# Staging k and q head by head in DRAM, and turning them from there in two 64-wide halves

## The chip, the cores and the metric

One core of one Trainium2 chip. The metric is the device time of one execution in microseconds (us). TensorE (PE) multiplies matrices, VectorE (DVE), ScalarE (ACT) and GpSimd (POOL) do the elementwise work, SyncE (SP) issues most of the transfers, and sixteen DMA engines move the data. GpSimd issues transfers too; those that change the number type (float32 to float16) all come from it.

## The reference

Attention with a bias by distance, followed by a two-layer network on its output. In the sizes of this case:

```python
# q, k, v: (8, 8, 576, 64) float32: 8 batch elements, 8 heads, 576 positions, 64 wide
scores = (1 / np.sqrt(64)) * np.matmul(q, k.transpose(0, 1, 3, 2))
scores = scores + bias_table[bucket].transpose(2, 0, 1)[None]   # bucket: by |i - j|
attn = softmax(scores)                                           # over the last axis
x = np.matmul(attn, v)           # then heads side by side: (4608 tokens, 512)
h = x @ w_in                     # (4608, 2048)
s = np.sin(alpha * h)
g = h + s * s / (alpha + 1e-09)
out = g @ w_out                  # (4608, 512) float32
```

The scores contract over the 64-wide head dimension, so TensorE needs k and q with that dimension on the partitions, the transpose of how they lie in DRAM.

## The kernel before, in words

The eight batch elements go through attention one after the other; the network follows some elements behind, in blocks of 512 tokens, and its matmuls are woven between those of the attention. The heads are taken in four pairs (`NP` = 4): a pair fills 128 partitions, the even head on 0 to 63, the odd one on 64 to 127.

The tiles `kT` and `qT` hold the turned k and q of one element, `[128, 4 pairs, 576]` in float16. There are two of each, used in turn by even and odd elements. For elements 0 and 1, and for q of element 2, the inputs are loaded to SBUF and turned on TensorE. For the rest (k of elements 2 to 7, q of elements 3 to 7, eleven tensors) two steps do it:

- `stage` (line 1238): a transfer issued by GpSimd reads one element's k or q from its input, casts it to float16 and writes it to a DRAM tensor `staged`, with the eight heads of one position side by side (576 rows of 512). `stage` is the only writer of it.
- `turn_staged` (line 1244): one transposing transfer issued by SyncE reads these 576 rows and writes `kT` or `qT`, whole.

After it, `corners` (line 1248) copies the last 64 positions of k into `kd`, and the score matmuls (lines 1364, 1395 and 1405) read `kT`, `qT` and `kd`.

SyncE issues in a fixed order, and its transfers go through one queue (q1): the staged turns, the transposing transfers `turn_x` (line 1478) which turn the attention's output into `xT`, the input of the network, and the stores of the results (lines 1626, 1645, 1652). GpSimd likewise issues in a fixed order (queue q0): early loads, then per element the loads of v and the two `stage` copies.

The order on each engine is written out by hand: the list `LINE` gives for every engine the sequence of its tasks, and a planner (`_Plan.run`) only walks along it. A task waits for its semaphores when its turn comes; what stands behind it on the same engine waits too. `turn_staged` of element t depends on its own `stage` and on the last score matmul of element t - 2, whose tile it overwrites:

```python
c = add("SP", 2.8, E("turn_staged", t, kind), pipe=3.3, prio=1, pkt=37, flow=True,
        deps=[staged[t, kind]] + last_qk[t - 2])
```

Of the kernel before, what the change touches and what calls it, by code (L numbers as in the profile page):

```python
# [9 lines left out]
F16 = mybir.dt.float16  # L10
# [4 lines left out]
T, H, S, D = 8, 8, 576, 64  # L15
NB, DM, FF, NT = 32, 512, 2048, 4608
NP = H // 2
# [4 lines left out]
def _blocks(sizes):  # L22

    at = [0]
    for n in sizes:
        at.append(at[-1] + n)
    assert at[-1] == NT
    return list(zip(at, at[1:]))


def _bucket_table(max_abs: int) -> np.ndarray:
    n = np.arange(max_abs)
    half = 16
    is_small = n < half
    log_ratio = np.log(np.maximum(n, 1).astype(np.float32) / half) / np.log(128 / half)
    large = half + (log_ratio * (half - 1)).astype(np.int32)
    large = np.minimum(large, 31)
    return np.where(is_small, n, large)
# [5 lines left out]
class _Ring:  # L44


    def __init__(self, n):
        self.n = n
        self.users = []
# [1031 lines left out]
class _Ops:  # L1081


    def __init__(self, ctx, tc, q, k, v, bias_table, moe_w_in, moe_w_out, moe_alpha, out):
        self.nc = nc = tc.nc
        self.q, self.k, self.v, self.out = q, k, v, out
        self.tab_in, self.w_in_in, self.w_out_in, self.alpha_in = (
            bias_table, moe_w_in, moe_w_out, moe_alpha)
        sgl = ctx.enter_context(tc.tile_pool(name="sgl", bufs=1))
        self.tp = ctx.enter_context(tc.tile_pool(name="tp", bufs=1))  # L1090
        ps = ctx.enter_context(tc.tile_pool(name="ps", bufs=1, space=bass.MemoryType.PSUM))
        self.acc = ps.tile([128, 8, 512], F32, name="acc")

        self.blk = _blocks(OPT["blk"])
        self.staged = [nc.dram_tensor(f"staged_{n}", [T, S, H * D], F16, kind="Internal")
                       for n in "kq"]
        bt = _bucket_table(256)

        cst = np.zeros((128, 784), dtype=np.float16)
        for a in range(4):  # L1100
            for y in range(488):
                cst[4 * bt[min(255, abs(y - 231 - 8 * a))] + a, y] = 1.0
            cst[a::4, 488 + a] = 1.0

        sub = np.repeat(np.eye(NB, dtype=np.float32), 4, axis=1)
        sub[NB - 1] -= 1.0
        cst[0:NB, 496:752] = sub.view(np.float16)
        cst[0:16, 752:784] = np.eye(16, dtype=np.float32).view(np.float16)
        self.cst_h = nc.inline_tensor(cst, "cst")
        self.ident_h = nc.inline_tensor(np.eye(128, dtype=np.float16), "eye")  # L1110

        self.kT = [sgl.tile([128, NP, S], F16, name=f"kT{i}") for i in range(2)]
        self.qT = [sgl.tile([128, NP, S], F16, name=f"qT{i}") for i in range(2)]
        self.kd = [sgl.tile([128, NP, 128], F16, name=f"kd{i}") for i in range(2)]
        self.vs = [sgl.tile([128, 4, H, 66], F16, name=f"v{i}") for i in range(2)]
        self.vt = [sgl.tile([128, NP, 130], F16, name=f"vt{i}") for i in range(2)]
        self.ur = [sgl.tile([128, 1088], F16, name=f"ur{i}") for i in range(OPT["nr"])]
        self.n_r = 0
        self.us = [sgl.tile([128, 320], F16, name=f"us{i}") for i in range(2)]
        self.xT = sgl.tile([128, NP, XR + 64], F16, name="xT")  # L1120
        self.toep = sgl.tile([128, H, 384], F16, name="toep")
        self.mt = sgl.tile([128, NP, 192], F16, name="mt")
        self.cst = sgl.tile([128, 784], F16, name="cst_sb")
        self.pick = self.cst[:, 0:492]
        self.ident = sgl.tile([128, 128], F16, name="ident")
        self.sub = self.cst[0:NB, 496:752].bitcast(F32)
        self.id32 = self.cst[0:16, 752:784].bitcast(F32)
        self.tab = sgl.tile([NB, H], F32, name="tab")
        self.e16 = sgl.tile([128, H], F16, name="e16")
        self.eb = sgl.tile([128, 4, H], F16, name="eb")  # L1130
        self.e_sb = sgl.tile([128, 392], F16, name="e_sb")
        self.w_in = sgl.tile([128, 4, FF], F16, name="w_in16")
        self.w_out = sgl.tile([128, NF, DM], F16, name="w_out16")
        self.a16 = sgl.tile([16, 128], F32, name="a16")
        self.alphaT = sgl.tile([128, NF], F32, name="alphaT")
        self.tmp_a = sgl.tile([128, NF], F32, name="tmp_a")
        self.inv_a = sgl.tile([128, NF], F32, name="inv_a")
        raw = self.toep[0:96].rearrange("p h n -> p (h n)").bitcast(F32)
        self.raw = [raw[:, 768 * i:768 * i + 768].rearrange("p (h n) -> p h n", h=2)
                    for i in range(2)]  # L1140
        self.blank = self.cst[:, 0:256]
        self.sums = sgl.tile([128, 2, 2, NF // 2, 256], F16, name="sums")
        self.wt = sgl.tile([128, 4, NF // 2, 256], F16, name="wt")
        self.touched = sgl.tile([1, 2], F32, name="touched")
        self.g = {}
# [91 lines left out]

    def stage(self, t, kind):
        src = (self.k, self.q)[kind]
        self.nc.gpsimd.dma_start(  # L1240
            out=self.staged[kind].ap()[t].rearrange("s (h d) -> s h d", h=H),
            in_=src[t].rearrange("h s d -> s h d"))

    def turn_staged(self, t, kind):
        dst = (self.kT, self.qT)[kind][t % 2]
        self.nc.sync.dma_start_transpose(out=dst[:, :, 0:S], in_=self.staged[kind].ap()[t])

    def corners(self, t, pairs):
        lo, hi = pairs[0], pairs[-1] + 1
# [455 lines left out]
```

## Time and profile before

| | |
|---|---|
| median of three runs | 373.29 us (373.19 to 374.27) |
| profiled execution | span 370.6 us; its own time beside the span is not given, and the median lies 2.7 us above the span |
| TensorE busy | 356.4 us (96%) |
| VectorE, ScalarE busy | 318.8 us, 318.4 us (86% each) |
| GpSimd busy | 87.9 us (24%) |
| bytes moved by DMA | 40.86 MB in 152415 packets |

The page of the profile lists the busy time of each engine, the traffic of each DMA queue, the chain of work that ended last, the costliest groups of instructions, and the issues of transfers with their time from issue to landing. A queue's share is the sum of the times of its packets over sixteen engines' time; it goes above 100% where packets overlap in an engine. Further views used below: the timeline of one engine, the instructions of one line or one tile, and the traffic in a cut of the span.

### The profile page before, as it was taken

How to read it: one execution, taken by the hardware profiler on the slowest of the kernel's cores; microseconds unless marked ns; L12 is line 12 of the kernel's file. 1: busy time of each engine (PE TensorE's matmuls, PEld its weight loads, DVE VectorE, ACT ScalarE, POOL GpSimd, SP SyncE). 2: the span in 40 equal slices, each digit the busy share in tenths (PEclk: the TensorE clock that was granted, in tenths of full speed). 3: DMA queues.
4: the chain of work that ended last, by engine and by line, in shares of the span. 5: the costliest groups of instructions: out<-in, count | busy, mean ns of one | idle time of the engine just before them, and what ended most of it. 6: DMA issues, size and time to landing. Idle time of an engine off the chain costs nothing.

```text
span 370.6 us, 10525 instructions
## 1 busy us (share of the span) xinstructions
PE 356.4 (96%) x4379; PEld 245.9 (66%) x4379; DVE 318.8 (86%) x711; ACT 318.4 (86%) x424; POOL 87.9 (24%) x105
## 2 busy tenths in 40 slices
PE   4969999999999999999999999999999999999996
PEld 3647546764666569755788987666965766745675
DVE  2679999999989998989998998899879997989733
ACT  5897999999999999999998999999899798476310
POOL 8895523085108000820050006200000000000000
PEclk9999999999999999999999999999999999999999
DMA  8999999899949954999799039907230012220014
GB/s 161 224 154 180 206 171 156 104 134 157 182 83 135 142 127 75 156 155 88 125 210 95 18 84 142 157 3 155 79 48 2 10 47 79 56 85 2 0 58 170
DMA packets 152415, 40.86 MB, mean 110 GB/s; under 512 B 134432, under 2 KB 151920, under 8 KB 152368
## 3 DMA queue, kind: packets, MB, share of 16 engines
q0 software_dynamic: 96656, 18.45, 60.2%
q1 hardware_dynamic: 55008, 21.22, 28.0%
q8 instruction: 34, 0.56, 0.6%
q10 hardware_dynamic: 704, 0.53, 0.6%
q14 instruction: 13, 0.11, 0.1%
HBM read 36.94 MB, written 15.93 MB: 143 GB/s over the span
## 4 chain that ended last, share of the span: by engine, by line
PE 87%; ACT 4%; POOL 3%; DMA 2%; DVE 2%; issue 1%; ACTq 0%; POOLq 0%; DVEq 0%
PE acc L1514 32%; PE acc L1611 26%; PE acc L1461 10%; PE acc L1405 9%; PE acc L1451 3%; PE acc L1558 3%; DMA wt<-in_k_dram 2%; PE acc L1364 2%; ACT s L1522 1%; PE acc L1395 1%; POOL mt L1292 1%; PE acc L1632 1%; DVE g L1543 1%; ACT u L1413 1%; POOL v L1219 1%
## 5 line engine op out<-in xcount | busy, mean ns | idle before, releaser
L1514 PE MATMUL acc<-xT,w_in 128*128 128x512 f16 (+3 forms) x704 | 134.2, 340 | 0.7 <-DVE g L1543 0.4
L1413 ACT ACTIVATE u<-acc 128x1024 f16<-128x1024 f32 x128 | 124.3, 1035 | 8.4 <-PE acc L1405 6.4
L1543 DVE SCALAR_TENSOR_TENSOR g<-s,inv_a,acc 128x512 f16<-128x512 f16 (+2 forms) x160 | 104.5, 691 | 8.6 <-ACT s L1527 6.5
L1522 ACT ACTIVATE s<-acc,alphaT 128x512 f16<-128x512 f32 (+2 forms) x144 | 93.2, 684 | 14.7 <-PE acc L1514 10.6
L1514 PEld LDWEIGHTS <-w_in 128*128 128x128 f16 x704 | 64.4, 98 | 55.8 <-DVE g L1543 1.8
L1611 PEld LDWEIGHTS <-g 128*128 128x128 f16 (+1 forms) x768 | 59.8, 96 | 18.0 <-issue 4.4
L1441 DVE TENSOR_TENSOR u<-u,toep 128x256 f16<-128x256 f16 (+1 forms) x128 | 59.4, 487 | 1.8 <-DMA toep<-e_sb 0.9
L1219 POOL DMA_DIRECT2D v<-in_v_dram x32 | 36.8, 1278 | 99.3 <-PE acc L1461 93.3
L1611 PE MATMUL acc<-w_out,g 128*128 128x256 f16 (+1 forms) x496 | 54.1, 271 | 0.0
L1405 PE MATMUL acc<-qT,kT 64*128 64x256 f16 x512 | 46.3, 279 | 3.9 <-DVE qT L1350 1.9
L1461 PE MATMUL acc<-v,u 128*128 128x65 f16 x1024 | 45.0, 193 | 0.1
L1527 ACT ACTIVATE s<-s 128x512 f16<-128x512 f16 (+2 forms) x67 | 41.4, 629 | 1.5
L1461 PEld LDWEIGHTS <-u 128*128 128x128 f16 x1024 | 40.6, 97 | 1.4 <-issue 0.5
L1611 PE MATMUL acc<-wt,g 128*128 128x256 f16 (+1 forms) x272 | 38.4, 272 | 0.0
L1611 PE MATMUL acc<-wt,sums 128*128 128x256 f16 (+1 forms) x272 | 34.6, 273 | 0.0
L1529 DVE TENSOR_TENSOR s<-s 128x512 f16<-128x512 f16 (+2 forms) x77 | 31.9, 422 | 2.6 <-ACT s L1522 2.3
L1472 DVE TENSOR_TENSOR xp<-acc,rden 128x256 f16<-128x256 f32 (+1 forms) x64 | 31.4, 491 | 2.2
L1405 PEld LDWEIGHTS <-kT 64*128 64x128 f16 x512 | 20.3, 96 | 16.1 <-issue 12.2
L1611 PEld LDWEIGHTS <-sums 128*128 128x128 f16 (+1 forms) x272 | 23.5, 97 | 7.9 <-issue 2.5
L1451 PE MATMUL acc<-vt,ut 128*128 128x130 f16 x128 | 28.3, 221 | 0.1
L1225 POOL DMA_DIRECT2D vt<-in_v_dram x16 | 14.1, 894 | 33.6 <-PE acc L1461 30.6
L1492 DVE COPY quarter<-acc 128x512 f32<-128x512 f32 x18 | 12.4, 687 | 9.3 <-PE acc L1611 4.7
(90 smaller groups left out, 361.6 us busy)
## 6 DMA issues: line engine op xcount, KB each, us to landing
out_dram<-quarter SPq DMA_DIRECT2D x32, 256.0 KB, 2.7
v<-in_v_dram POOLq DMA_DIRECT2D x32, 128.0 KB, 8.7
staged_k<-in_k_dram POOLq DMA_DIRECT2D x6, 576.0 KB, 10.8
staged_q<-in_q_dram POOLq DMA_DIRECT2D x5, 576.0 KB, 9.9
w_out<-in_moe_w_out_dram POOLq DMA_DIRECT2D x4, 512.0 KB, 8.7
w_in<-in_moe_w_in_dram POOLq DMA_DIRECT2D x4, 512.0 KB, 16.2
sums<-in_q_dram POOLq DMA_DIRECT2D x7, 144.0 KB, 5.6
out_dram<-outs SPq DMA_DIRECT2D x3, 256.0 KB, 2.0
```

Source lines behind the costliest of these rows:

```text
L1219: self.nc.gpsimd.dma_start(out=self.vs[t % 2][:, c, :, 0:D], in_=src)
L1405: self.nc.tensor.matmul(out=s[:, o:o + 256], lhsT=self.kT[t % 2][r, p, 128 * c:128 * c + 128], rhs=self.qT[t % 2][r, p, 256 * w:256 * w + ...
L1413: self.nc.scalar.activation(out=c["u"], in_=c["s"], func=AF.Exp, scale=0.125)
L1441: self.nc.vector.tensor_tensor(out=io, in0=io, in1=m, op=ALU.mult)
L1451: nc.tensor.matmul(out=c["av"][:, 130 * j:130 * j + 130], lhsT=tail, rhs=vt[:, p, :], start=True, stop=True, skip_group_check=True)
L1461: nc.tensor.matmul(out=c["av"][:, 130 * j + 65 * a:130 * j + 65 * a + 65], lhsT=l, rhs=vv[:, ch, 2 * p + a, 0:65], start=False, stop=True, ...
L1514: self.nc.tensor.matmul(out=c["h"][:, x:y], lhsT=self.w_in[:, j, 128 * f:128 * f + 128], rhs=self.xT[:, j, at:at + y - x], start=(j == 0 a ...
L1522: self.nc.scalar.activation(out=c["s"], in_=c["h"], func=AF.Sin, scale=self.alphaT[:, f:f + 1])
L1527: self.nc.scalar.activation(out=c["s"], in_=c["s"], func=AF.Square)
L1529: self.nc.vector.tensor_tensor(out=c["s"], in0=c["s"], in1=c["s"], op=ALU.mult)
L1543: self.nc.vector.scalar_tensor_tensor(out=o, in0=c["s"][:, x:y], scalar=self.inv_a[:, f:f + 1], in1=c["h"][:, x:y], op0=ALU.mult, op1=ALU.add)
L1611: self.nc.tensor.matmul(out=c[to][:, 256 * k:256 * k + 256], lhsT=a[r, 128 * k:128 * k + 128], rhs=b[r, :], start=to not in c["began"], st ...
```

## The change

`staged` becomes, per element, two halves (even and odd heads), and each half holds its four heads one after the other, each as 576 rows of 64: `[2, 4 * 576, 64]`. `stage` issues two copies in place of one, one for each half, with runs of 2048 numbers that are contiguous on both sides. `turn_staged` issues two transposes in place of one: each takes a half, seen as 2304 rows of 64, and writes it to 64 partitions of `kT` or `qT`, all four pairs in one row of 2304 columns. The planner's costs and the orders on the engines are the same.

```diff
-        self.staged = [nc.dram_tensor(f"staged_{n}", [T, S, H * D], F16, kind="Internal")
+        self.staged = [nc.dram_tensor(f"staged_{n}", [T, 2, NP * S, D], F16, kind="Internal")
                        for n in "kq"]
...
     def stage(self, t, kind):
         src = (self.k, self.q)[kind]
-        self.nc.gpsimd.dma_start(
-            out=self.staged[kind].ap()[t].rearrange("s (h d) -> s h d", h=H),
-            in_=src[t].rearrange("h s d -> s h d"))
+        n = S * D // 18
+        for a in range(2):
+            self.nc.gpsimd.dma_start(
+                out=bass.AP(tensor=self.staged[kind].ap().tensor, offset=(2 * t + a) * NP * S * D,
+                            ap=[[n, 18 * NP], [1, n]]),
+                in_=bass.AP(tensor=src.tensor, offset=src.offset + (t * H + a) * S * D,
+                            ap=[[2 * S * D, NP], [n, 18], [1, n]]))
 
     def turn_staged(self, t, kind):
         dst = (self.kT, self.qT)[kind][t % 2]
-        self.nc.sync.dma_start_transpose(out=dst[:, :, 0:S], in_=self.staged[kind].ap()[t])
+        for a in range(2):
+            self.nc.sync.dma_start_transpose(
+                out=dst[64 * a:64 * a + 64, :, :].rearrange("d p s -> d (p s)"),
+                in_=self.staged[kind].ap()[t, a])
```

## The prediction

> **What bounds the kernel now.** I read the page first (busy times, chain that ended last), then the waits, then what the change touches: the queues, the tiles, the timeline of SyncE.
>
> ```profile
> span 370.6 us, 10525 instructions
> PE 356.4 (96%) x4379; PEld 245.9 (66%) x4379; DVE 318.8 (86%) x711; ACT 318.4 (86%) x424; POOL 87.9 (24%) x105
> ...
> q0 software_dynamic: 96656, 18.45, 60.2%
> q1 hardware_dynamic: 55008, 21.22, 28.0%
> ...
> PE 87%; ACT 4%; POOL 3%; DMA 2%; DVE 2%; issue 1%; ACTq 0%; POOLq 0%; DVEq 0%
> ```
>
> TensorE bounds it: 356.4 of 370.6 us busy, 87% of the chain. At most 14.2 us could be gained without taking work from TensorE, and this change takes none away. So its upside is small whatever it does, and the question is whether the new transfers stay hidden. In the instructions of the two tiles and the list of transfers, the old ones are:
>
> ```profile
> L1240 POOL DMA_DIRECT2D staged_k<-in_k_dram x6: 2197/2232/2782, 37.8 to 189.6; - x6
> L1246 SPq DMA_TRANSPOSE kT<-staged_k x6: 2138/2751/4722, 55.5 to 219.0; - x6
> ```
>
> ```profile
> out_dram<-quarter SPq DMA_DIRECT2D x32, 256.0 KB, 2.7
> ...
> staged_k<-in_k_dram POOLq DMA_DIRECT2D x6, 576.0 KB, 10.8
> staged_q<-in_q_dram POOLq DMA_DIRECT2D x5, 576.0 KB, 9.9
> ...
> xT<-xp SPq DMA_TRANSPOSE x28, 2.9
> ...
> kT<-staged_k SPq DMA_TRANSPOSE x6, 5.3
> qT<-staged_q SPq DMA_TRANSPOSE x5, 5.4
> ```
>
> Eleven turns, each 5.3 or 5.4 us from issue to landing. Where they stand on SyncE (start, duration):
>
> ```profile
> 55.53 4.72 SPq L1246 DMA_TRANSPOSE kT<-staged_k  x1
> 68.55 1.20 SPq L1478 DMA_TRANSPOSE xT<-xp  x1
> 69.93 2.92 SPq L1246 DMA_TRANSPOSE kT<-staged_k  x1
> ...
> 218.98 2.29 SPq L1246 DMA_TRANSPOSE kT<-staged_k  x1
> ...
> 228.99 22.39 SPq L1626 DMA_DIRECT2D out_dram<-quarter  x3
> 251.49 2.46 SPq L1246 DMA_TRANSPOSE qT<-staged_q  x1
> ```
>
> The last turn (q of element 7) is issued at 251.49 and lands at about 256.9; the 64 score matmuls of element 7's full tiles, counted back from the end, begin at 259.2:
>
> ```profile
> L1405 PE MATMUL acc<-qT,kT x64: 269/269/280, 259.2 to 301.1; 64*128 64x256 f16 x64
> ```
>
> So the slack of that turn is 2.3 us, and behind it lie 370.6 - 259.2 = 111.4 us of work.
>
> **The stage step.** GpSimd's issue: 2.23 us each, eleven times, 24.5 us; after, 22 issues of 72 runs each. The nearest issue with few runs is a load of w_out:
>
> ```profile
> 22.14 0.78 POOL L1235 DMA_DIRECT2D w_out<-in_moe_w_out_dram  x1
> ```
>
> 22 x 0.78 = 17.2 us, a gain of 7 us on an engine that is busy 24%; bounds from -24.5 to +24.5 us, no path either way: 0. Behind each stage on GpSimd stand the v loads, which can only move by a microsecond or two. On the DMA engines the run gets longer (one packet carries 128 bytes now, 4096 then), so 11 x 4608 = 50688 of q0's 96656 packets become 22 x 72 = 1584. This too only matters if a turn waits for its stage; I take 0.
>
> **The turn step** decides. All transposing transfers of this kernel take whole units of 128 columns: 512 (4 x 128) for the staged turns, 640 (5 x 128) for `xT`. A cut inside a staged turn with nothing else in it shows the packets:
>
> ```profile
> DMA packets 792, 0.20 MB, mean 290 GB/s; under 512 B 792, under 2 KB 792, under 8 KB 792
> ## 3 DMA queue, kind: packets, MB, share of 16 engines
> q1 hardware_dynamic: 792, 0.20, 127.3%
> ```
>
> 0.20 MB / 792 = 256 bytes, one row of 128 numbers of two bytes. The cut is 0.7 us (60.5 to 61.2): 0.7 x 16 / 792 = 14.1 ns per packet on each engine. A whole turn is 2304 such packets, 144 on each engine, 2.0 us of its 5.3.
>
> The new source has rows of 64 numbers, half a unit. Nothing in the trace shows a transposing transfer with half a unit. If it isn't taken so, what is left is a plain transfer with the strides exchanged: 64 rows of 2304 numbers, in which neighbours lie 64 numbers (128 bytes) apart in DRAM. The trace shows what a plain transfer pays for: one packet for one contiguous run (64 float16 on the staged side, 128 bytes, here beside w_out's longer ones):
>
> ```profile
> q0 software_dynamic: 5664, 0.72, 126.1%
> ```
>
> 0.72 MB / 5664 = 127 bytes, in the cut from 60 to 69 us. With exchanged strides the run is one number: 64 x 2304 = 147456 packets of two bytes for each half, 9216 on each engine, against 144 before.
>
> [...]
>
> I take the exchanged strides. **The price of a two-byte packet** isn't in the trace. From below: the completion words of four bytes, 32 of them alone in a cut of 0.21 us (259.75 to 259.96):
>
> ```profile
> DMA packets 32, 0.00 MB, mean 1 GB/s; under 512 B 32, under 2 KB 32, under 8 KB 32
> ## 3 DMA queue, kind: packets, MB, share of 16 engines
> q1 hardware_dynamic: 32, 0.00, 7.0%
> ```
>
> 0.07 x 16 x 0.21 us / 32 = 7.35 ns. From above: GpSimd's queue over the whole span, 0.602 x 16 x 370.6 us / 96656 = 36.9 ns per packet, mostly 128-byte ones of the staging itself and in traffic. Between them lies the 14.1 ns of the 256-byte packets. I take 14.1 ns: same queue, same DRAM tensor as source, same destination, and I expect the packet, not its bytes, to set the price. Then one transfer takes 9216 x 14.1 ns = 129.9 us (67.7 to 340 by the bounds).
>
> [...]
>
> **What it puts on the path.** There are 22 such transfers, all in SyncE's queue, and nothing covers them: the six turns of k stand (219.0 - 55.5) / 5 = 33 us apart on average, and an element's four transfers now take 4 x 130 = 520 us. Queued behind them on SyncE and in q1 are the `xT` transposes (the network's next block waits for them on TensorE, and through TensorE's fixed order the attention too) and the stores. TensorE, VectorE and ScalarE wait at the first score matmul of each later element.
>
> - Until the first turn is issued: 55.5 us, as before.
> - 22 x 129.9 = 2858 us. Each turn's own start and landing overlap its neighbour's in the queue: 0.
> - Between elements the queue runs dry while SyncE waits for the work that stands before its next turn. In the trace of before the distance from the landing of an element's last turn to the next turn's issue is, as a bound, up to about 27 us (k of element 7: 218.98 + 5.3 = 224.3; q is issued at 251.5), taken for five places at most 135 us in all; most of that work is done now while the turns run. The 22.39 us at the three stores before q7 stay. I take 60 us, bounds 0 and 135.
> - Behind the last turn: 111.4 us.
> - Around the span: 2.7 us (373.29 - 370.6).
>
> Sum: 55.5 + 2858 + 60 + 111.4 + 2.7 = 3088 us, said as 3100. By the lower price 1490 us of transfers and 1660 us in all; by the upper one 7480 and, with 135 between, 7785, said as 7700.
>
> **The rivals.** (1) The half unit is taken as a transposing transfer: 4608 packets of 128 bytes a tensor, at 14.1 ns 288 on each engine, 4.1 us in place of 2.0, and a second issue on SyncE of 1.2 us (the shortest, `xT`'s above). A turn lands 2 to 4 us later; only q of element 7 has as little as 2.3 us. For it: the change is written with the transposing instruction. Against it: not one such transfer in the trace. Time: 373 us, between 371.5 (some of the staging's contention gone) and 376. This is the not-slower side; it decides when half a unit costs no more than a whole one, which keeps a turn within about 8 us. (2) Exchanged strides, but the sixteen engines read the same 128-byte line at the same moments, since each takes four of the 64 numbers of every line, and they hinder one another: above 36.9 ns, so over 7.7 ms. For it: in traffic, packets in q0 took 36.9 ns, 2.6 times the 14.1. [...] (3) The read side is paid below the completion words' 7.35 ns: under 1660 us. For it: packets overlap (127.3% above). Against: 7.35 ns is the shortest there is here.
>
> **How the numbers follow.** Exchanged strides inside the bounds: 0.82. Rival 2: 0.06, rival 3: 0.04, rival 1: 0.08, of which faster 0.03, same 0.04, slower 0.01. Range 1660 to 7700 us, holding the 0.82. About 0.3% is what a measurement tells from no change here; faster 0.03, same 0.04, slower 0.93.
>
> **What would show it.** Right: the entries of line 1246's successor are no longer transposing ones but plain ones; q1 has about 22 x 147456 = 3.2 million packets, two bytes each, or as many as the profiler keeps; landing in the hundreds of microseconds; TensorE's busy time still near 356 us but its share near 12%; the first large waits of TensorE are for `kT` and `qT`, and the chain goes over DMA. Wrong: transposing entries of 128-byte packets that land within 10 us (rival 1); or the stage step, if turns wait for it instead.

## The result, and the profile after

The changed kernel takes 4430.43 us (median of four runs, 4424.83 to 4449.39); the kernel before, run beside it, 373.78 us (373.19 to 374.69). The ratio is 11.86, with a 95% interval of 11.82 to 11.90. The forecast was 3100 us, between 1660 and 7700: the side and the kind of thing are right, the time is 1330 us short. The profiled execution took 4426.38 us at a span of 4424.2 us. (In the experiments "stage alone", "whole units" and "short runs" some of the four runs took 2 to 8% longer than the others at a lower clock, 0.925 to 0.970 against 0.953 to 0.982; their times below are those of the shorter ones, two, one and two of them, and from the profiles of the last two kernels, which are of a longer run, only kinds and counts are read.)

The page of the changed kernel: busy times, the granted clock over the span (one digit for each fortieth), the queues, the chain.

```profile
span 4424.2 us, 10558 instructions
PE 382.5 (9%) x4379; PEld 259.3 (6%) x4379; DVE 320.8 (7%) x711; ACT 320.7 (7%) x424; POOL 77.4 (2%) x116
...
PEclk7555555655565555555555555555555655565559
...
DMA packets 3321647, 40.87 MB, mean 9 GB/s; under 512 B 3303400, under 2 KB 3320888, under 8 KB 3321336
...
q1 hardware_dynamic: 3273696, 21.22, 178.1%
q0 software_dynamic: 47200, 18.46, 4.1%
...
another core or an unknown queue 74%; SPq 16%; PE 6%; DMA 2%; DVE 1%; POOL 0%; issue 0%; ACT 0%; DVEq 0%; POOLq 0%; ACTq 0%
```

The engines do the same work as before (TensorE 382.5 us against 356.4; the clock granted to it was 0.543 on average, 1.000 before), but it is spread over twelve times the span. The bytes are as good as the same (40.87 MB, 40.86 before). q1 has 3273696 packets where it had 55008. Take away from both the turns: before, 11 x 2304 = 25344 of 256 bytes; after, 22 x 147456 = 3244032 of two bytes. 29664 are left in both. So every turned number crosses as a packet of its own. Most of the chain stands under "another core or an unknown queue" (what the profile calls a wait it can't follow) and under SyncE's queue, in which the turns lie.

The list of transfers of the changed kernel (KB each, median us from issue to landing), and the row of the turns of k among the tile's instructions (duration of the issue in ns: shortest, median, longest):

```profile
staged_k<-in_k_dram POOLq DMA_DIRECT2D x12, 288.0 KB, 14.1
kT<-staged_k SPq DMA_DIRECT2D x12, 288.0 KB, 288.5
staged_q<-in_q_dram POOLq DMA_DIRECT2D x10, 288.0 KB, 15.9
qT<-staged_q SPq DMA_DIRECT2D x10, 288.0 KB, 376.0
```

```profile
L1251 SPq DMA_DIRECT2D kT<-staged_k x12: 607/91386/199646, 55.3 to 3527.5; - x12
```

Eleven transposing transfers have become 22 plain ones, although the kernel calls the transposing function. A landing of 288 to 376 us holds the wait behind the other half in the queue; in "one half" below, without that other half, it is 192 to 197 us. The price of one transfer by itself is read from a cut in which nothing else moves (4000 to 4100 us):

```profile
DMA packets 79792, 0.16 MB, mean 2 GB/s; under 512 B 79792, under 2 KB 79792, under 8 KB 79792
...
q1 hardware_dynamic: 79792, 0.16, 194.9%
```

0.16 MB / 79792 = 2 bytes. On each of sixteen engines a packet ends every 100 x 16 / 79792 = 20.05 ns; the share of 194.9% says that two are under way on each engine, so that one takes 39 ns. A transfer of 9216 packets on each engine takes 9216 x 20.05 ns = 184.8 us.

SyncE's timeline shows what this does to all that is queued behind (start, duration):

```profile
55.28 200.43 SPq L1251 DMA_DIRECT2D kT<-staged_k  x2
255.79 184.91 SPq L1485 DMA_TRANSPOSE xT<-xp  x1
440.88 200.24 SPq L1251 DMA_DIRECT2D kT<-staged_k  x2
641.22 187.51 SPq L1485 DMA_TRANSPOSE xT<-xp  x3
828.78 0.58 SPq L1633 DMA_DIRECT2D out_dram<-quarter  x1
829.46 188.93 SPq L1251 DMA_DIRECT2D qT<-staged_q  x2
...
4121.93 186.00 SPq L1485 DMA_TRANSPOSE xT<-xp  x2
```

An issue now lasts up to 199.6 us, as long as a whole transfer, and SyncE stands at it that long. The chain's "SPq" (16%) is this. Hence TensorE's waits, in the view of the waits (total, times, longest):

```profile
PE acc L1412 <- DMA qT<-staged_q: 1452.3, 6, 548.2
...
DVE kd L1261 <- DMA kT<-staged_k: 741.0, 4, 189.6
...
PE acc L1521 <- DMA xT<-xp: 732.6, 2, 368.1
```

TensorE waits for q (1452.3 us), for `xT` behind the turns (732.6 us), and by way of `kd` (741.0 us on VectorE) for k. The two stretches of the span in the view by windows (length, then busy time of TensorE, its weight loads, VectorE, ScalarE and GpSimd, granted clock, DMA share, GB/s):

```profile
55.30:4307.90 4252.60, 227.14 (x2638) 154.33 (x2637) 193.85 (x430) 201.28 (x259) 41.42 (x56) 0.53 1.87 6
4307.90:4424.20 116.30, 109.88 (x1063) 75.13 (x1062) 84.90 (x176) 72.18 (x104) 0.00 (x0) 0.97 0.20 52
```

The sum: 55.3 us to the first turn; 22 x 184.8 = 4066 us; 4252.6 - 4066 = 187 us in which no turn was under way or one ran slower than in the cut; 116.3 us behind the last packet. Together 4424.2.

### The profile page after: what moved, and what is told of

Read it like the earlier page. It is cut to its first block, busy times and chain, and to the rows that moved or that the text cites. A ratio compares the mean times of both kernels' runs of the same rounds, so it can differ in the third digit from the quotient of the medians.

```text
span 4424.2 us, 10558 instructions
## 1 busy us (share of the span) xinstructions
PE 382.5 (9%) x4379; PEld 259.3 (6%) x4379; DVE 320.8 (7%) x711; ACT 320.7 (7%) x424; POOL 77.4 (2%) x116
## 2 busy tenths in 40 slices
DMA packets 3321647, 40.87 MB, mean 9 GB/s; under 512 B 3303400, under 2 KB 3320888, under 8 KB 3321336
## 3 DMA queue, kind: packets, MB, share of 16 engines
q1 hardware_dynamic: 3273696, 21.22, 178.1%
## 4 chain that ended last, share of the span: by engine, by line
another core or an unknown queue 74%; SPq 16%; PE 6%; DMA 2%; DVE 1%; POOL 0%; issue 0%; ACT 0%; DVEq 0%; POOLq 0%; ACTq 0%
SPq L1251 8%; SPq L1485 4%; SPq L1633 4%; PE acc L1521 2%; PE acc L1618 2%; PE acc L1468 1%; PE acc L1412 1%; DMA v<-in_v_dram 1%; DMA w_in<-in_moe_w_in_dram 0%; DMA vt<-in_v_dram 0%; PE acc L1565 0%; PE acc L1458 0%; DMA w_out<-in_moe_w_out_dram 0%; DVE g L1550 0%
## 5 line engine op out<-in xcount | busy, mean ns | idle before, releaser
L1412 PE MATMUL acc<-qT,kT 64*128 64x256 f16 x512 | 53.1, 301 | 1830.5 <-DMA qT<-staged_q 1452.3
L1521 PE MATMUL acc<-xT,w_in 128*128 128x512 f16 (+3 forms) x704 | 138.6, 347 | 733.1 <-DMA xT<-xp 732.6
L1478 DVE RECIPROCAL rden<-acc 128x4 f32<-128x4 f32 (+1 forms) x64 | 11.9, 185 | 1119.9 <-PE acc L1468 1119.6
L1261 DVE TENSOR_TENSOR kd<-kT 64x256 f16<-64x256 f16 x12 | 3.4, 284 | 741.1 <-DMA kT<-staged_k 741.0
## 6 DMA issues: line engine op xcount, KB each, us to landing
staged_k<-in_k_dram POOLq DMA_DIRECT2D x12, 288.0 KB, 14.1
```

The lines of the kernel that those rows point to most:

```text
L1412: self.nc.tensor.matmul(out=s[:, o:o + 256], lhsT=self.kT[t % 2][r, p, 128 * c:128 * c + 128], rhs=self.qT[t % 2][r, p, 256 * w:256 * w + ...
L1521: self.nc.tensor.matmul(out=c["h"][:, x:y], lhsT=self.w_in[:, j, 128 * f:128 * f + 128], rhs=self.xT[:, j, at:at + y - x], start=(j == 0 a ...
```

## The experiments

In every diff the kernel named first is the one that loses lines. "Stage alone", "whole units", "short runs" and "stage spread" were run four times and "short and spread" ten times; the others, whose effects are large, once. The theory at the outset: the turn is a plain transfer of single numbers, its price is one per packet, and the stage is worth nothing. The rivals: the engines disturb one another on the lines that they read, or the stage has a part in the loss.

### What the turn costs

**Turn alone.** From the kernel before, with its stage: eight transfers of 64 columns, one for each head. All of the output is computed.

```diff
-        self.nc.sync.dma_start_transpose(out=dst[:, :, 0:S], in_=self.staged[kind].ap()[t])
+        for h in range(H):
+            self.nc.sync.dma_start_transpose(
+                out=dst[64 * (h % 2):64 * (h % 2) + 64, h // 2, :],
+                in_=self.staged[kind].ap()[t, :, 64 * h:64 * h + 64])
```

> The stage of before, and the turn head by head from it: eight transposes of 576 rows of 64 (1024 bytes apart in DRAM) for each tensor. All numbers as in the reference. The same 294912 two-byte packets per tensor as in the changed kernel. Theory (the count of packets sets the time): 4400 to 4500 us. Rival (the layout of the rows sets the price of a packet): another price than 20 ns, so for instance 3200 us at 14.1 ns or 7800 us at 36.9 ns.

Measured: 4357.87 us. A cut from 100 to 200 us:

```profile
q1 hardware_dynamic: 77278, 0.15, 176.6%
```

The old stage and rows of 64 that lie 1024 bytes apart give 20.7 ns per packet and nearly the whole loss. The new stage isn't needed for it. What makes this kernel 73 us shorter than the changed one, the old stage or the other cut of the turn, wasn't separated.

**Whole units.** From the changed kernel: two transposing transfers, but each takes 256 columns of 576 rows. The order of the bytes is wrong; their number is the same.

```diff
-            self.nc.sync.dma_start_transpose(
-                out=dst[64 * a:64 * a + 64, :, :].rearrange("d p s -> d (p s)"),
-                in_=self.staged[kind].ap()[t, a])
+            rows = self.staged[kind].ap()[t, a].rearrange("(s x) d -> s (x d)", x=NP)
+            self.nc.sync.dma_start_transpose(out=dst[:, 2 * a:2 * a + 2, :], in_=rows[:, 0:256])
```

> The new stage and two transposing transfers for each tensor, as in the change, but each sees its half as 576 rows of 256, whole units of 128 numbers (the numbers land in a wrong order). Theory (rows of 64 are what throws the transfer out of its transposing form): 373 to 376 us, 22 transposing entries on SyncE of 1.2 to 3 us. Rival (two transfers in place of one, each into a part of the tile, are what costs): several hundred us or more above before.

Measured: 399.79 us. The turns in the tile's view:

```profile
L1252 SPq DMA_TRANSPOSE kT<-staged_k x12: 1234/1498/6643, 55.3 to 254.5; - x12
```

Two transfers a tensor are still transposing ones when the rows are 256 wide. So it is the 64-wide row, and not the second transfer, that leaves the transposing form. The time isn't that of before, though: some 26 us are lost with the turn cheap. Those are followed up further down.

**One half.** Only the first half is turned; the other half of `kT` and `qT` holds old numbers.

```diff
-        for a in range(2):
+        for a in range(1):
             self.nc.sync.dma_start_transpose(
```

> The changed kernel without the second of the two turns (the odd heads' half of kT and qT keeps old numbers). Theory (the 22 transfers stand one behind the other on the path, 9216 packets on each engine at 20.06 ns = 184.9 us each): 4424 - 11 x 184.9 = 2390 us of span. Rival (part of the transfers was covered, or the time lies in waits between them): clearly more than 2390.

Measured: 2398.37 us. The list of transfers:

```profile
kT<-staged_k SPq DMA_DIRECT2D x6, 288.0 KB, 196.7
```

The cost is linear in the transfers: (4430.4 - 2398.4) / 11 = 184.7 us for each that is left out, the same as by the packets of the cut. Nothing covers them.

**Own lines.** The same packets to the same places, but neighbouring partitions read 4608 bytes apart, in place of two. The numbers in the tiles are other ones.

```diff
-            self.nc.sync.dma_start_transpose(
-                out=dst[64 * a:64 * a + 64, :, :].rearrange("d p s -> d (p s)"),
-                in_=self.staged[kind].ap()[t, a])
+            self.nc.sync.dma_start(
+                out=dst[64 * a:64 * a + 64, :, :].rearrange("d p s -> d (p s)"),
+                in_=bass.AP(tensor=self.staged[kind].ap().tensor, offset=2 * t * NP * S * D,
+                            ap=[[NP * S, D], [D, NP * S]]), allow_slow_non_contiguous=True)
```

> The changed kernel with the same plain two-byte packets, 128 bytes apart along a row of the tile, but each partition starts 4608 bytes behind the last, so that no two DMA engines read the same 128 bytes at the same moment (the numbers read are wrong ones). Theory A (a packet has a fixed price on its engine, 20 ns): 4430 us. Theory B (the sixteen engines hinder one another on one line of DRAM): falls to 14.1 ns or less a packet, 3250 us or less.

Measured: 4438.77 us, and from 100 to 200 us:

```profile
q1 hardware_dynamic: 79675, 0.16, 194.9%
```

79675 packets against 79792, within 0.2% of the changed kernel's rate. Reading the same line of DRAM costs nothing that can be seen here: the prediction's second rival falls. The plain call costs what the transposing call does here.

**Four bytes.** Half as many packets, each of four bytes (two float16 taken as one float32). Each half tile gets pairs of numbers that lie otherwise.

```diff
+        at = self.staged[kind].ap()[t].rearrange("a r d -> a (r d)").bitcast(F32)
         for a in range(2):
-            self.nc.sync.dma_start_transpose(
-                out=dst[64 * a:64 * a + 64, :, :].rearrange("d p s -> d (p s)"),
-                in_=self.staged[kind].ap()[t, a])
+            self.nc.sync.dma_start(
+                out=dst[64 * a:64 * a + 64, :, :].rearrange("d p s -> d (p s)").bitcast(F32),
+                in_=bass.AP(tensor=at.tensor, offset=at.offset + a * NP * S * D // 2,
+                            ap=[[1, D], [D, NP * S // 2]]), allow_slow_non_contiguous=True)
```

> The changed kernel with the same bytes moved in packets of four bytes in place of two, half as many (the numbers land wrongly). Theory A (price for each packet, whatever it holds): 22 x 4608 x 20.06 ns = 2034 us of transfers and 357 us beside, 2390 us. Rival (price by bytes): 4430 us.

Measured: 1292.08 us. From 110 to 140 us:

```profile
q1 hardware_dynamic: 51041, 0.20, 189.0%
```

30 x 16 / 51041 = 9.4 ns for a packet of four bytes on each engine, less than half of the 20.05 ns for two. A fixed price per packet, as I had it, would have given 2390 us. So the theory falls in this point: something in a two-byte packet costs extra. The shared lines are out ("Own lines"); the write to the tile was tried next, and how many engines there are for it.

**Eight engines.** A half as eight transfers of eight neighbouring partitions. All of the output is computed.

```diff
-            self.nc.sync.dma_start_transpose(
-                out=dst[64 * a:64 * a + 64, :, :].rearrange("d p s -> d (p s)"),
-                in_=self.staged[kind].ap()[t, a])
+            for i in range(0, D, 8):
+                self.nc.sync.dma_start(
+                    out=dst[64 * a + i:64 * a + i + 8, :, :].rearrange("d p s -> d (p s)"),
+                    in_=self.staged[kind].ap()[t, a, :, i:i + 8].rearrange("r d -> d r"),
+                    allow_slow_non_contiguous=True)
```

> The same packets, but each transfer cut into eight of 8 partitions, so that eight DMA engines carry everything, if the split goes by the outermost count. Numbers as in the reference. Theory A (20 ns on each engine): twice the time for the transfers, 22 x 369.8 + 357 = 8490 us. Theory C (one shared source hands out packets for all engines, one each 1.25 ns): about 4430 us, packets on an engine at 10 ns.

Measured: 15439.95 us. From 500 to 600 us:

```profile
q1 hardware_dynamic: 20462, 0.04, 94.0%
```

Neither 8490 us (half the engines, each as before) nor 4430 us (all numbers at one rate wherever they go). A packet now ends every 100 / 20462 us = 4.9 ns in all, against 1.25 ns in the changed kernel. If eight engines carry it, each ends one every 39 ns. The records don't name an engine; 94.0%, about half of 194.9%, fits eight with two under way on each.

**Two queues.** The second half is issued by ScalarE, in a queue of its own, so that both halves move at once. All of the output is computed.

```diff
-            self.nc.sync.dma_start_transpose(
+            (self.nc.scalar if a else self.nc.sync).dma_start(
                 out=dst[64 * a:64 * a + 64, :, :].rearrange("d p s -> d (p s)"),
-                in_=self.staged[kind].ap()[t, a])
+                in_=self.staged[kind].ap()[t, a].rearrange("r d -> d r"),
+                allow_slow_non_contiguous=True)
```

> The second half of each turn is issued from ScalarE's queue in place of SyncE's. Numbers as in the reference. The trace of the changed kernel shows two packets of 39 ns under way on an engine at any time. If two under way is a limit of a queue, two queues give four, and the transfers take half: about 2400 us. If it is a limit of the engine, or of what hands the packets out: about 4430 us, each packet then 78 ns from start to end or the halves one after the other.

Measured: 2732.43 us. From 100 to 200 us:

```profile
q10 hardware_dynamic: 79155, 0.16, 95.0%
q1 hardware_dynamic: 79153, 0.16, 89.9%
```

Two queues move 158308 packets in the time of 79792: on the same sixteen engines a packet now ends every 10.1 ns, and one takes 184.9% x 16 x 100 us / 158308 = 18.7 ns in place of 39. So the engines weren't the limit at 20 ns. The reason that I had expected isn't it: there are still about two packets under way on each engine (95.0% + 89.9%) and not four, but each takes half as long. With the two halves the writes go to partitions 64 to 127 as well as 0 to 63; the second queue came in by the same edit.

That led to this theory: the price of a two-byte write goes by the partitions that are written side by side. In all, a packet ends every 0.63 ns into the 128 partitions of "Two queues", every 1.25 ns into the 64 of the changed kernel, and every 4.9 ns into eight neighbouring ones. For these it is less elsewhere in "Eight engines"; from 3000 to 3100 us:

```profile
q1 hardware_dynamic: 24119, 0.05, 98.4%
```

Here it is 100 us / 24119 = 4.1 ns, and why is open.

**Every fourth.** The test of it: as "Eight engines", but each transfer takes every fourth partition in place of eight neighbours. The same packets, the same number of partitions in a transfer.

```diff
-            for i in range(0, D, 8):
+            for i in (0, 1, 2, 3, 32, 33, 34, 35):
                 self.nc.sync.dma_start(
-                    out=dst[64 * a + i:64 * a + i + 8, :, :].rearrange("d p s -> d (p s)"),
-                    in_=self.staged[kind].ap()[t, a, :, i:i + 8].rearrange("r d -> d r"),
+                    out=dst[64 * a + i:64 * a + i + 29:4, :, :].rearrange("d p s -> d (p s)"),
+                    in_=self.staged[kind].ap()[t, a, :, i:i + 29:4].rearrange("r d -> d r"),
                     allow_slow_non_contiguous=True)
```

> As the kernel with eight engines (15440 us), the same 2304 packets on each of eight engines for a transfer, but a transfer takes every fourth partition (0, 4, ... 28) in place of eight neighbours. Numbers as in the reference. [...]

Measured: 5575.43 us, 2.8 times faster than neighbouring partitions. From 700 to 800 us:

```profile
q1 hardware_dynamic: 61972, 0.12, 90.3%
```

A packet ends every 1.6 ns in place of 4.9, with nothing changed but the partitions of a transfer (and with them the places that are read, which made 0.2% in "Own lines"). So which partitions are written side by side decides; of the choices there are, the runs try only these two, a half, and both halves at once. If eight engines carry it, each ends a packet every 100 x 8 / 61972 us = 12.9 ns from one queue, where one ended every 20.05 ns in the changed kernel, so it isn't the second queue as such that "Two queues" gains by. An engine ended a packet every 10.1 ns in "Two queues"; what holds it at 12.9 ns here wasn't separated. Nor was it tried why two bytes cost more than four do.

### What the stage costs

**Stage alone.** The changed kernel's stage; then one transposing transfer of the same bytes, 512 wide, as before. The order of the bytes in the tiles is wrong.

```diff
-        for a in range(2):
-            self.nc.sync.dma_start_transpose(
-                out=dst[64 * a:64 * a + 64, :, :].rearrange("d p s -> d (p s)"),
-                in_=self.staged[kind].ap()[t, a])
+        rows = self.staged[kind].ap()[t].rearrange("a (s x) d -> (a s) (x d)", x=H)
+        self.nc.sync.dma_start_transpose(out=dst[:, :, 0:S], in_=rows)
```

> The new stage (two copies with long runs) with the single turn of before, which reads the same bytes as 576 rows of 512. The numbers in kT and qT of the later elements are therefore in a wrong order; the amount of work is that of before. My theory (the turn alone costs the time; the stage step is worth 0): 373 to 374 us, staged copies landing in about 10 to 15 us. Rival (the staging carries part of the loss, because its runs use fewer DMA engines or land late): more than 380 us, with waits of SyncE for the staged copies.

Measured: 404.49 and 405.28 us, 1.083 times the kernel before (1.079 to 1.087). The stage by itself costs about 31 us, where I had put nothing. The page, the transfers, and the waits:

```profile
PE 365.9 (91%) x4379; PEld 251.0 (62%) x4379; DVE 319.3 (79%) x711; ACT 318.9 (79%) x424; POOL 77.2 (19%) x116
...
q0 software_dynamic: 47200, 18.46, 47.4%
...
PE 75%; DMA 14%; POOL 3%; ACT 3%; DVE 3%; issue 2%; POOLq 0%; DVEq 0%
```

```profile
staged_k<-in_k_dram POOLq DMA_DIRECT2D x12, 288.0 KB, 14.4
```

```profile
PE acc L1519 <- DMA xT<-xp: 16.7, 2, 8.6
PE acc L1456 <- DMA vt<-in_v_dram: 7.3, 1, 7.3
```

DMA's share of the chain goes from 2% to 14%. TensorE waits 16.7 us for `xT` and 7.3 us for `vt`, and in its busy time 9.5 us are added (365.9 against 356.4) at a granted clock of 0.953 where it was 1.000. 24.0 + 9.5 = 33.5 us, against a span that is 32.5 us longer (403.1 - 370.6). GpSimd issues faster, as forecast (77.2 us busy against 87.9), and that is worth nothing. The place, on the chain (start, length) and in TensorE's timeline:

```profile
78.70 14.34 DMA xT<-xp
...
163.66 12.43 DMA vt<-in_v_dram
...
211.67 16.59 DMA xT<-xp
```

```profile
93.08 4.00 PE L1519 MATMUL acc<-xT,w_in 128*128 128x512 f16 x9 [8.64 <-DMA xT<-xp]
```

Transfers of 14 and 17 us. The landings of all 28 `xT` transfers, first in the kernel before, then in this one, have the same middle and another end:

```profile
DMA to landing us min/median/max: 2.6/2.9/5.9
```

```profile
DMA to landing us min/median/max: 2.6/3.1/16.6
```

What is beside them: the staging in the cut from 84 to 92 us, first this kernel, then the kernel before.

```profile
q0 software_dynamic: 732, 0.72, 199.2%
```

```profile
q0 software_dynamic: 9745, 1.23, 243.4%
```

A packet of q0 took 1.992 x 16 x 8 us / 732 = 348 ns on average, against 32 ns before, and fewer bytes were moved. The records show why: the written runs of 2048 were joined to runs of 12288 numbers, twelve packets of 24576 bytes for a copy, at about 2 us each. The theory: the long packets of the staging hold up those of `xT`. Or: few engines carry the long copies, and these are just late. The next three kernels shorten the packets, or spread them, or both. Each is "stage alone" with another stage, so its output is in the same wrong order.

**Short runs.** Runs of 512 numbers, 288 packets of 1024 bytes a copy; the head still is the outermost of its counts.

```diff
-                            ap=[[2 * S * D, NP], [n, 18], [1, n]]))
+                            ap=[[2 * S * D, NP], [n, 18], [1, n]]), max_dma_last_dim=n)
```

> The same kernel, with the outermost count of the staging copies left at 4 and only the runs cut: 288 packets of 1024 bytes for a copy in place of 12 of 24576. If a long packet that holds its engine is the cause: 373 to 378 us. If it is the few engines that carry all of a copy's bytes, which a transposing transfer over all sixteen then waits for: 395 us or more, with copies landing as late as before the cut (14 us).

Measured: 385.9 us, 1.032 times the kernel before (1.030 to 1.034), between the two times that I had named. GpSimd's queue:

```profile
q0 software_dynamic: 71488, 18.53, 50.7%
```

The edit did more than shorten the runs. The copies are 22 x 288 = 6336 of these packets, but by the packet records 20608 of them have four bytes, where "stage alone" has 2392 such.

**Stage spread.** Outermost a count of 32, then the four heads, with runs of 1152 numbers: 128 packets of 2304 bytes a copy.

```diff
-        n = S * D // 18
+        n = S * D // 32
...
-                            ap=[[n, 18 * NP], [1, n]]),
+                            ap=[[n, 32], [S * D, NP], [1, n]]),
...
-                            ap=[[2 * S * D, NP], [n, 18], [1, n]]))
+                            ap=[[n, 32], [2 * S * D, NP], [1, n]]))
```

> As the kernel with the new stage alone (single turn, numbers in a wrong order), but each stage copy goes 32 times over the four heads in runs of 1152 numbers, so that the outermost count is 32 in place of 4; 128 packets of 2304 bytes for a copy in place of 12 of 24576. If the form of the staging copies (12 long packets on few engines) is what cost about 30 us there: 373 to 376 us, and staged copies landing in well under 10 us. If moving the staging in two copies costs by itself: 400 us or more.

Measured: 382.76 us, 1.022 times (1.018 to 1.025), again between the two times named. The transfers, then the chain:

```profile
staged_k<-in_k_dram POOLq DMA_DIRECT2D x12, 288.0 KB, 10.1
```

```profile
53.69 16.79 DMA kT<-staged_k
...
79.99 7.65 DMA xT<-xp
...
157.52 10.15 DMA xT<-xp
...
200.75 8.87 DMA xT<-xp
```

The copies land in 10.1 us in place of 14.4, about as fast as before, and still `xT` is late, by less, and so is a turn: `kT` has 6% of this chain, `xT` 7%, and `kT` is not among the larger parts of the chain in "stage alone". Both go through SyncE's queue. So late copies aren't the whole of it.

**Short and spread.** Two copies to the new places, in runs of 64 numbers: 2304 packets of 128 bytes a copy, as the kernel before has them.

```diff
-        n = S * D // 18
...
-                            ap=[[n, 18 * NP], [1, n]]),
+                            ap=[[D, S], [S * D, NP], [1, D]]),
...
-                            ap=[[2 * S * D, NP], [n, 18], [1, n]]))
+                            ap=[[D, S], [2 * S * D, NP], [1, D]]))
```

> As the kernel with the new stage alone (single turn, numbers in a wrong order): the same two copies into the same head-by-head places, but in runs of 64 numbers and with an outermost count of 576, so 2304 packets of 128 bytes for a copy, as short as before the change. If the length of GpSimd's packets, behind which the packets of SyncE's transposes wait on each DMA engine, is what cost the 2.2% with 2304-byte packets and 8.3% with 24576-byte ones: 373 to 376 us, as before, and no wait of TensorE for xT over 1 us. If two copies in place of one, or the new places in DRAM, cost by themselves: 380 us or more.

Measured: 374.04 us against 374.19, 0.999 times (0.998 to 1.001). The page and the transfers:

```profile
q0 software_dynamic: 96832, 18.45, 60.9%
...
PE 82%; DVE 6%; ACT 5%; POOL 2%; issue 2%; DMA 2%; ACTq 0%; DVEq 0%; POOLq 0%
```

```profile
staged_k<-in_k_dram POOLq DMA_DIRECT2D x12, 288.0 KB, 8.9
```

The whole loss of the stage is gone with the long runs. Neither the second copy nor the new places cost anything. Between the two spread kernels only the run differs, and with it the outermost count (32 and 576): 2304 bytes cost 2.2%, 128 bytes nothing. By the packet records the 256-byte packets of SyncE's transposing transfers took 26.0 ns on average before, 32.2 in "stage alone", 30.7 in "stage spread" and 26.4 here: beside long packets of the other queue they get slower. "Short runs" has packets shorter than "stage spread" and loses more, 3.2%. The way a copy is spread may count beside the length, but its many packets of four bytes may too; that wasn't separated. The slower packets fit the theory, but no run here shows one packet waiting for another on an engine. None of these kernels is faster than the one before.

## Why the prediction was right, and where it was wrong

**What bounds the kernel; the side.** Right. The old turns were hidden, there was little to be gained, and nothing covered the new ones. "One half" shows the cost in proportion to the transfers.

**The turn step, its kind.** Right. "I take the exchanged strides": 22 plain transfers of 147456 packets of two bytes, in number as forecast. It was an estimate: no transfer of the trace before had rows of 64. "Whole units" shows the row of 64 as what decides: rows of 64 were plain transfers, rows of 256 transposing ones. The first rival falls, as no 128-byte transposing packets exist. The second falls by "own lines". The third falls too: 20.05 ns lies above 7.35.

**The price of a two-byte packet.** Wrong in size, and this is nearly the whole miss: 14.1 ns was taken, 20.05 measured. 22 x 9216 x 5.95 ns = 1206 us of the 1330. The step that failed is the choice within the bounds: "same queue, same DRAM tensor as source, same destination, and I expect the packet, not its bytes, to set the price". "Four bytes" refutes it: 9.4 ns. The 14.1 ns of a row of 128 numbers of a transposing transfer said nothing of a single number's price, and that price follows the partitions: with both halves under way ("two queues") it was halved to 10.1 ns, and "every fourth" changed it by the choice of partitions alone, from 4.9 to 1.6 ns between packets in all. Why two bytes cost more than four stays open.

That the time lies inside the range is in part luck. The bounds, 7.35 and 36.9 ns, are the times that packets took (share by count); 14.1 ns, like 20.05, is the time from one packet's end to the next on an engine, and the 256-byte packet took 18 ns by its 127.3%. Measured as the bounds were, a two-byte packet took 39 ns, more than the upper one, and 22 x 9216 x 39 ns would have been 7900 us. The transfers took half of it because two packets were under way at a time (194.9%), which the prediction weighed only in its third rival.

**Between the turns.** 60 us was taken, with bounds of 0 and 135; 187 us were measured above 22 undisturbed transfers. By the packet records no turn was under way for about 129 us of it, inside the bounds and at their upper end: the work that stands before an element's next turn wasn't done while the turns ran, since much of it waited for `xT`, behind the same turns. The rest is transfers that ran slower than in the cut (187.3 us each on average; 192.3 us in the first pair, beside the staging); the sum left this out.

**The ends.** 55.3 us for 55.5; 116.3 for 111.4, of which 2.5 us lie between the last packet and the first score matmul (4310.43 us) and the rest fits TensorE's clock of 0.97 there; 2.2 us around the span for 2.7.

**The stage step.** Wrong: "I take 0". Alone it costs 31 us, eight per cent of the kernel. The prediction saw that the run gets longer and only asked whether a turn would wait for its stage. It didn't ask what longer packets do to the transfers of the other queue; `xT`, with nothing else changed about it, came late (landings of up to 16.6 us, 5.9 before). The count was off too: not 72 runs but 12 a copy, since these runs, contiguous on both sides, were joined to 24576 bytes, 264 packets in place of 1584. How much of this loss is left in the changed kernel, where `xT` waits for the turns in any case, isn't shown; "turn alone", with the old stage, is 73 us shorter, but its turns are cut otherwise too.

**What would show it.** The entries of the turns, the number of packets and the landings came as named. The chain goes over the turns by way of SyncE's queue and of waits that the profile can't follow, not under the name of DMA (2%). TensorE's busy share is 9% and not 12%, as the span is longer, and its busy time is 382.5 and not 356 us: behind the last wait it worked slowly for a while. In the first work behind the last turn, from 4310.4 to 4315.3 us, the granted clock was 0.51, and from there to 4321.0 it was 1.00.

## What to carry to other kernels

Look in the profile whether a transposing transfer still is one: rows of 64 numbers turned it into one packet per number here, where rows of 256 and 512 did not, and that was 70 times the price (a tensor's turn went from 5.3 us to 2 x 184.8 = 370 us). Where the price of a packet has to be guessed, ask on both sides what it touches: its reading, its writing, and which partitions it writes side by side. And a longer run isn't better by itself: beside packets of 24576 bytes of one queue, the 256-byte packets of another took 32.2 ns in place of 26.0, so look what else moves at that time.

## What the runs showed of the hardware that I had not expected

- Two bytes cost more than four: 20.05 ns per packet on each engine against 9.4, into the same 64 partitions.
- The price of a two-byte write goes by the partitions written side by side: 4.1 and 4.9 ns between packets in all for eight neighbouring ones (two cuts), 1.6 for eight that lie four apart, 1.25 for 64, 0.63 for all 128 at once.
- Beside long packets on GpSimd's queue the 256-byte ones on SyncE's took longer (32.2 ns on average beside packets of 24576 bytes, 30.7 beside 2304, 26.4 beside 128): copies in packets of 24576 bytes cost 8.3%, of 2304 bytes, spread more widely, 2.2%, and of 128 bytes nothing. Packets of 1024 bytes, with some 18000 more of four bytes beside them, cost 3.2%.
- The clock granted to TensorE was 0.543 on average over a span in which it mostly waited, 0.51 in the first 5 us behind the last wait and 1.00 in the 6 us after that; its work of 356.4 us took 382.5.
